# Scores of the pooled attention as 64-row products of even and odd tokens, with that order of tokens kept to the store

## The chip, the cores and the metric

The kernel runs on one core of a Trainium2 chip. The metric is the device time of one execution in microseconds (us). The core's engines are TensorE (PE in the profile, with PEld for its weight loads), VectorE (DVE), ScalarE (ACT), GpSimd (POOL) and SyncE (SP), whose queue issues all the DMA transfers here. Each engine works its own instructions in the order in which the program gives them.

## The reference

Eight batches of eight heads attend from 576 queries (64 dimensions) to 72 keys and values, each the mean of eight neighbours. The result, 4608 tokens by 512, goes through two dense layers with a squared ReLU between them.

```python
k_p = k.reshape(B, H, Sp, pool, D).mean(axis=3)
v_p = v.reshape(B, H, Sp, pool, D).mean(axis=3)
scores = scale * np.matmul(q, k_p.transpose(0, 1, 3, 2))
scores = scores - np.max(scores, axis=-1, keepdims=True)
attn = np.exp(scores)
attn = attn / (np.sum(attn, axis=-1, keepdims=True) + 1e-09)
attn_out = np.matmul(attn, v_p)
x = attn_out.transpose(0, 2, 1, 3).reshape(B * S, H * D)
h = np.maximum(x @ w_in, 0.0)          # 512 -> 2048
out = h * h @ w_out                    # 2048 -> 512
```

## The kernel before

The 4608 tokens are worked in 12 chunks of CH = 384. As a batch has 576 tokens, chunks 1, 4, 7 and 10 hold tokens of two batches (two segments of 192 in `segments`, lines 289 to 296), the others of one.

The main loop (lines 684 to 705) runs over 16 blocks of 128 hidden features for each chunk, in steps (c, fc). In step s TensorE gets twelve h products of 384 columns (`hidden`, line 502), then what the attention has for this step, then nine o products of 512 columns for the block two steps back (`project`, line 539; the lag is LAG = 2). Products of float32 accuracy are made from three products of fp32r parts, high times high, high times low and low times high; `split` (lines 127 to 129) makes the parts, the high one by a copy on ACT, the low one by a subtraction on DVE. Chunk 0, and the scores and the av products, use plain float32 operands.

The attention of a chunk is done for four pairs of heads, spread over the steps of the chunks before it (STEADY, line 87, gives the first step of each pair and the offsets of its stages from there). From chunk 2 on a pair's stages are these:

- `transpose_q` (line 309): four TensorE transposes put q of both heads into one PSUM bank `qps`, two neighbouring tokens at a time, so that the even token of each two stands on partitions 0 to 63 and the odd one on 64 to 127. The `then` part (lines 319 to 331) is the split: for each parity ACT copies the high part to its own 64 partitions of `st` and DVE writes the low part to the other 64. In `st` each token then has a column of 128 rows, half of it high and half low, in the order of the sequence.
- `scores` (line 335), one step later: for each head the products of `st` with `kl` and `kh`, the transposed pooled keys, which stand on both halves of the partitions. A product over 128 rows so sums the high and the low half. The scores of head i go to bank i of `sps`, 72 keys by 384 tokens, and ACT copies them to `sc`.
- `exponents` and the four stages behind it (lines 359 to 397): GpSimd takes maxima and sums over the 72 keys, ACT the exponentials, and the sums go over DRAM to be inverted in a compact form; `fetch_reciprocals` (line 392) broadcasts them from DRAM to the 64 partitions of each head in `rb`.
- `weigh_values` (line 472), eight steps after the transposes: `av` is the product of the exponents with the pooled values, the two heads on two halves of the output columns of the array; DVE multiplies it with `rb` and `split` makes `xh` and `xl`, the chunk's tokens for the h products.

At the end of a chunk `store` (lines 552 to 556) copies three tiles of 128 tokens out of PSUM and sends each with one DMA transfer to consecutive rows of the output.

In one step the order on TensorE is h, transposes and scores, av, o. Every transpose of q from chunk 3 on falls into a step with an av; the scores stand alone between the last h and the first o. The scores of chunks 0 and 1 are made otherwise (`token_scores`, line 408): in float32, with the tokens as stationary operand and 64 rows for each parity.

The lines that a sentence can't say are these of `scores`, line 343 and 344, the products that the change replaces:

```python
for j, kk in enumerate((kl, kh)):
    PE.matmul(ss[i][:SP_, o:o + n], lhsT=kk[:, h * SP_:(h + 1) * SP_], rhs=st[:, i, o:o + n], start=j == 0, stop=j == 1)
```

Of the kernel before, what the change touches and what calls it, by code (L numbers as in the profile page):

```python
# [9 lines left out]
F32 = mybir.dt.float32  # L10
# [4 lines left out]
ALU = mybir.AluOpType  # L15
# [22 lines left out]
def pooled_attn_relu2_ffn(  # L38
# [16 lines left out]
    PE, DVE, ACT, GP, SP = (InOrder(tc, e) for e in (nc.tensor, nc.vector, nc.scalar, nc.gpsimd, nc.sync))  # L55
    B, H, S, D = q.shape
# [3 lines left out]
    P = 128  # L60
    POOL = 8
    SP_ = S // POOL
# [3 lines left out]
    CH = 384  # L66
    QT = 96
    NQ = CH // QT
# [32 lines left out]
    ps_a = ctx.enter_context(tc.tile_pool(name="ps_a", bufs=3, space=bass.MemoryType.PSUM))  # L101
# [9 lines left out]
    for n in range(0, P, 32):  # L111
        rows = slice(n, n + 32)
# [3 lines left out]
    dma = SP.dma_start  # L116
# [10 lines left out]
    def split(hi, lo, src, eng=None):  # L127
        ACT.copy(hi, src)
        (eng or DVE).tensor_tensor(lo, src, hi.bitcast(F32), op=ALU.subtract)
# [5 lines left out]
    def w_tile(dt, name):  # L135
        return wts.tile([P, 2, 512], dt, name=name, tag="w", bufs=2 * NFC + 1)

    halves = {}

    def half_tile(kind, name):  # L140

        if kind not in halves:
            halves[kind] = w_tile(F32, name)
            return halves[kind][:, 0, :]
        return halves.pop(kind)[:, 1, :]
# [35 lines left out]
    kv, kf, loaded = {}, {}, {}  # L181
# [107 lines left out]
    def segments(c):  # L289
        t, segs = c * CH, []  # L290
        while t < (c + 1) * CH:
            b = t // S
            n = min((b + 1) * S, (c + 1) * CH) - t
            segs.append((b, t - c * CH, n))
            t += n
        return segs
# [12 lines left out]
    def transpose_q(c, p):  # L309


        pt = ps_a.tile([P, 512], F32, name=f"qps_{c}_{p}", tag="a")
        blocks = pt[:, :CH].rearrange("p (i t s) -> p i t s", i=2, s=QT)
        qt = loaded.pop(("q", c, p))
        for i in range(2):
            for t in range(NQ // 2):
                PE.transpose(blocks[:, i, t, :], qt[:, i, t * 2 * D:(t + 1) * 2 * D], ident[:QT, :QT])

        def then():
            if c < 2:  # L320
                st = live[c, p] = half_tile("s", f"st_{c}_{p}")[:, :CH]
                ACT.copy(st, pt[:, :CH])
                return
            st = live[c, p] = sb.tile([P, 2, CH], F32R, name=f"st_{c}_{p}", tag="st", bufs=STB)
            order = "p i (s t two) -> p i t s two" if len(segments(c)) == 1 else "p i (t s two) -> p i t s two"
            cols = st.rearrange(order, two=2, s=QT)
            halves = [(slice(i * D, (i + 1) * D), slice((1 - i) * D, (2 - i) * D), i) for i in range(2)]
            for own, oth, i in halves:
                ACT.copy(cols[own, :, :, :, i], blocks[own])
            for own, oth, i in halves:  # L330
                DVE.tensor_tensor(cols[oth, :, :, :, i], blocks[own], cols[own, :, :, :, i].bitcast(F32), op=ALU.subtract)

        return then

    def scores(c, p):

        st = live.pop((c, p))
        ss = [ps_a.tile([P, 512], F32, name=f"sps_{c}_{p}_{i}", tag="a") for i in range(2)]
        for i in range(2):
            h = 2 * p + i  # L340
            for b, o, n in segments(c):
                kh, kl, _ = kv[b]
                for j, kk in enumerate((kl, kh)):
                    PE.matmul(ss[i][:SP_, o:o + n], lhsT=kk[:, h * SP_:(h + 1) * SP_], rhs=st[:, i, o:o + n], start=j == 0, stop=j == 1)

        def then():
            sc = sb.tile([SP_, 2, CH], F32, name=f"sc_{c}_{p}", tag="sc", bufs=SCB)
            mx = reduced("mx", c, p)
            for i in range(2):
                ACT.copy(sc[:, i, :], ss[i][:SP_, :CH])  # L350
                GP.partition_all_reduce(mx[i], sc[:, i, :], channels=SP_, reduce_op=bass_isa.ReduceOp.max)
            live[c, p] = (sc, mx)

        return then

    def reduced(kind, c, p):
        return [sb.tile([SP_, CH], F32, name=f"{kind}_{c}_{p}_{i}", tag="mx", bufs=3) for i in range(2)]
# [34 lines left out]
    def fetch_reciprocals(c, p):  # L392
        sc, rd = live.pop((c, p))
        rb = sb.tile([P, CH], F32, name=f"rb_{c}_{p}", tag="rb", bufs=2)
        for i in range(2):
            dma(rb[i * D:(i + 1) * D, :], rd[i:i + 1, :].broadcast_to([D, CH]))
        live[c, p] = (sc, rb)


# [72 lines left out]
    def weigh_values(c, p):  # L472

        if p == 0 and c == 0:
            x0.extend(w_tile(F32, f"x_{c}_{i}")[:, :, :CH] for i in range(2))
        elif p == 0:
            xts[c] = (sb.tile([P, NPAIR, CH], F32R, name=f"xh_{c}", tag="xh", bufs=2),
                      sb.tile([P, NPAIR, CH], F32R, name=f"xl_{c}", tag="xl", bufs=2))
        sc, rb = live.pop((c, p))
        av = ps_a.tile([P, 512], F32, name=f"av_{c}_{p}", tag="a")  # L480
        for b, o, n in segments(c):
            for i in range(2):
                PE.matmul(av[i * D:(i + 1) * D, o:o + n], lhsT=kv[b][2][:, 2 * p + i, :], rhs=sc[:, i, o:o + n],
                                 start=True, stop=True)

        def then():
            if c == 0:
                ACT.copy(x0[p // 2][:, p % 2, :], av[:, :CH])
                return
            xh, xl = xts[c]  # L490
            if c == 1:
                split(xh[:, p, :], xl[:, p, :], av[:, :CH])
                return
            DVE.tensor_tensor(rb, av[:, :CH], rb, op=ALU.mult)
            split(xh[:, p, :], xl[:, p, :], rb)

        return then
# [41 lines left out]
    def project(c, fc):  # L539
        if fc == 0:  # L540
            accs[c] = [ps_o.tile([P, 512], F32, name=f"o_{c}_{t}", tag=f"o{t}") for t in range(NTT)]
        g, key = gts.pop((c, fc)), ("o", fc)
        for t in range(NTT):
            tt = slice(t * P, (t + 1) * P)
            if c == 0:
                prods = [(g[:, tt], wf[key])]
            else:
                prods = [(g[x][:, tt], wt[key][:, w, :]) for x, w in ((0, 0), (0, 1), (1, 0))]
            for i, (a, w) in enumerate(prods):
                PE.matmul(accs[c][t], lhsT=a, rhs=w, start=fc == 0 and i == 0, stop=fc == NFC - 1 and i == len(prods) - 1)  # L550

        def store():
            for t in range(NTT):
                ob = sb.tile([P, DM], F32, name=f"ob_{c}_{t}", tag="ob", bufs=OB)
                ACT.copy(ob, accs[c][t])
                dma(out[c * CH + t * P:c * CH + (t + 1) * P, :], ob)

        return store if fc == NFC - 1 else None

# [58 lines left out]
    for p in range(NPAIR):  # L618
        token_normalise(0, p)
        after = [token_scores(0, p + 2)] if p + 2 < NPAIR else []  # L620
        if p:
            weigh_values(0, p - 1)()
        keep_busy(IDLE[1])
        if p == 2:
            for key in first_keys:
                magnitude(key)
        token_turn(0, p)()
        for f in after:
            f()
    to_float32(*first_keys)  # L630
    weigh_values(0, NPAIR - 1)()
    for hf in range(2):
        at(0, transpose_k, 1, hf)
# [4 lines left out]
    t = 1e9  # L638
    for key in reversed(keys):
        t = min(t - 1 / RATE, need[key] - 1 - MARGIN)  # L640
# [23 lines left out]

    ready = {0, 1}
    stages = (transpose_q, scores, exponents, send_sums, fetch_sums, reciprocals, fetch_reciprocals, weigh_values)
    for c in range(1, NCH):
        first, offsets = EARLY if c == 1 else STEADY
# [5 lines left out]
        for p in range(NPAIR):  # L674
            s = c * NFC + first[p]
# [5 lines left out]

    last = (to_float32, split_weights)
    on_pe = (transpose_k, transpose_q, scores, token_scores, token_turn, weigh_values)
    for s in range(-PRO, len(steps) + LAG):
        todo = work.get(s, [])
# [50 lines left out]
```

## Time and profile before

| what | us |
|---|---|
| median of three runs | 964.42 |
| lowest and highest of them | 963.8, 966.72 |
| the profiled execution | 964.33 |
| its span, from the first to the last instruction | 962.6 |
| TensorE matmuls busy | 946.1 |
| VectorE busy | 615.0 |
| ScalarE busy | 451.5 |
| GpSimd busy | 348.8 |

The profile is taken in one execution; "busy" is the time in which an engine has at least one instruction under way. TensorE's instructions overlap in its pipeline and their ends are modelled, so that what one of them costs is read from the distance between two starts, not from its duration. A row of the timeline has the start, the time to the end of its last instruction, the engine, the operation, output and inputs by their names in the program (buffer numbers left out), rows and columns, and how many equal instructions are merged; the idle time before it and what ended it stand in brackets. Line L34 is the helper that issues every instruction, so that rows are told apart by the names of the tiles.

### The profile page before, as it was taken

To read this page: it belongs to the slowest core of one execution; us is meant where nothing else is said; L and a number is where in the kernel's file an instruction comes from. 1 tells how busy PE (TensorE), PEld (TensorE's weight loads), DVE (VectorE), ACT (ScalarE), POOL (GpSimd) and SP (SyncE) were. 2 spreads that over 40 slices of the span, in tenths; PEclk is the share of its full clock that TensorE was granted. 3 is DMA by queue.
4 is the path that set the end of the run, shared out by engine and by line. 5 is a ranking of instruction groups with operands and counts; after the bars stand their busy time and mean duration, and the time that the engine had idled before them with its cause. 6 is when DMAs were issued, how large, how long until landed. Compare 5 with 4: busy or idle time off the path is not lost.

```text
span 962.6 us, 13481 instructions
## 1 busy us (share of the span) xinstructions
PE 946.1 (98%) x4944; PEld 803.6 (83%) x4944; DVE 615.0 (64%) x1028; ACT 451.5 (47%) x909; POOL 348.8 (36%) x215
## 2 busy tenths in 40 slices
PE   7899999999999999999999999999999999999998
PEld 6456668888888888888888888888888888888997
DVE  7889886667865566677765656767776565453221
ACT  3789776754444344444344344434443434532322
POOL 3800144444444434344353444344443534440000
PEclk9799999999999999999999999999999999999999
DMA  9963112113112112112112112112211110100000
GB/s 256 319 237 116 61 33 78 35 50 98 52 31 77 32 34 67 48 52 82 52 44 77 30 35 79 38 30 69 82 50 39 68 32 18 58 10 9 33 1 34
DMA packets 51651, 63.65 MB, mean 66 GB/s; under 512 B 13936, under 2 KB 32192, under 8 KB 51584
## 3 DMA queue, kind: packets, MB, share of 16 engines
q1 hardware_dynamic: 51584, 62.78, 21.2%
q8 instruction: 39, 0.64, 0.3%
q14 instruction: 28, 0.23, 0.1%
HBM read 53.08 MB, written 9.68 MB: 65 GB/s over the span
## 4 chain that ended last, share of the span: by engine, by line
PE 88%; DVE 5%; DMA 4%; ACT 2%; issue 1%; SPq 0%; ACTq 0%; DVEq 0%
PE o L34 41%; PE h L34 39%; PE av L34 3%; PE sps L34 3%; DVE wf_o L34 2%; DVE wf_i L34 1%; PE qps L34 1%; DMA raw_o<-in_moe_w_out_dram 1%; DMA v<-in_v_dram 1%; DMA k<-in_k_dram 1%; ACT te L34 1%; DMA vv<-in_v_dram 1%; DMA raw_i<-in_moe_w_in_dram 1%; DVE tm L34 1%; DVE w_i L34 1%
## 5 line engine op out<-in xcount | busy, mean ns | idle before, releaser
L34 PE MATMUL h<-xh,w_i 128*128 128x384 f32 x1488 | 416.9, 341 | 0.0
L34 PE MATMUL o<-w_o,gh 128*128 128x512 f32 x1056 | 334.8, 398 | 0.0
L34 PEld LDWEIGHTS h<-xh,w_i 128*128 128x128 f32 x1488 | 272.8, 188 | 10.6 <-issue 1.4
L34 POOL PARTITION_ALL_REDUCE tot<-sc x80 | 201.4, 2564 | 210.1 <-issue 199.6
L34 PE MATMUL h<-xl,w_i 128*128 128x384 f32 x744 | 249.9, 336 | 0.0
L34 PEld LDWEIGHTS o<-w_o,gh 128*128 128x128 f32 x1056 | 192.4, 188 | 51.9 <-issue 16.5
L34 POOL PARTITION_ALL_REDUCE mx<-sc x80 | 117.8, 1519 | 287.1 <-ACT sc L34 287.1
L34 DVE TENSOR_TENSOR gl<-r,gh 128x384 fp32r<-128x384 f32 x176 | 143.5, 815 | 109.1 <-ACT gh L34 108.9
L34 PE MATMUL o<-w_o,gl 128*128 128x512 f32 x528 | 209.1, 396 | 0.0
L34 DVE TENSOR_TENSOR r<-r 128x384 f32<-128x384 f32 x160 | 105.6, 660 | 109.1 <-ACT r L34 108.8
L34 ACT CAST gh<-r 128x384 fp32r<-128x384 f32 x176 | 90.4, 514 | 150.3 <-DVE r L34 149.8
L34 PEld LDWEIGHTS h<-xl,w_i 128*128 128x128 f32 x744 | 139.7, 188 | 10.6 <-issue 2.9
L34 ACT ACTIVATE r<-h 128x384 f32<-128x384 f32 x192 | 94.2, 491 | 100.5 <-PE h L34 99.1
L34 PEld LDWEIGHTS o<-w_o,gl 128*128 128x128 f32 x528 | 99.1, 188 | 22.1
L34 DVE TENSOR_TENSOR st<-qps,st 64x384 fp32r<-64x384 f32 x80 | 60.8, 760 | 59.1 <-ACT st L34 58.3
L34 ACT CAST st<-qps 64x384 fp32r<-64x384 f32 x80 | 59.5, 744 | 56.9 <-PE qps L34 56.5
L34 ACT CAST xh<-rb 128x384 fp32r<-128x384 f32 x40 | 20.5, 513 | 94.6 <-DVE rb L34 94.6
L34 ACT ACTIVATE sc<-sc 72x384 f32<-72x384 f32 x80 | 39.7, 525 | 46.4 <-DVE sc L34 46.4
L34 DVE TENSOR_REDUCE vp<-v 72x64 f32<-72x512 f32 x48 | 51.0, 1062 | 0.0
L34 PE MATMUL av<-sc,vp 72*64 72x384 f32 (+1 forms) x256 | 45.6, 436 | 3.6 <-ACT sc L34 2.1
L34 PE MATMUL o<-wf_o,r 128*128 128x512 f32 x96 | 44.4, 598 | 0.0
L34 DVE TENSOR_REDUCE kp<-k 96x64 f32<-96x512 f32 x42 | 43.8, 1043 | 0.2 <-DMA k<-in_k_dram 0.2
(82 smaller groups left out, 702.1 us busy)
## 6 DMA issues: line engine op xcount, KB each, us to landing
k<-in_k_dram SPq DMA_DIRECT2D x48, 192.0 KB
out_dram<-ob SPq DMA_DIRECT2D x36, 256.0 KB
raw_i<-in_moe_w_in_dram SPq DMA_DIRECT2D x16, 512.0 KB
raw_o<-in_moe_w_out_dram SPq DMA_DIRECT2D x16, 512.0 KB
v<-in_v_dram SPq DMA_DIRECT2D x56, 144.0 KB
rb<-rd SPq DMA_DIRECT2D x80, 96.0 KB
q<-in_q_dram SPq DMA_DIRECT2D x30, 192.0 KB
q<-in_q_dram SPq DMA_DIRECT2D x32, 96.0 KB
```

What stands on the lines that cost most here:

```text
L34: return lambda *a, **k: self.tc.keep_in_program_order(f(*a, **k))
```

## The change

From chunk 2 on the split of q keeps the parities where the transposes put them: `st` gets the high parts in its first half and the low ones in its second, each over 128 partitions, even tokens on partitions 0 to 63 and odd ones on 64 to 127. The scores become products over 64 rows, three terms for each parity (high keys by low queries, low by high, high by high), alternating between the two halves of the array; bank j of `sps` now holds parity j, with both heads one behind the other. A product has 192 columns in a chunk of one batch and 96 in one of two. The order of tokens (even ones, then odd ones, each by transposed blocks) stays through the softmax, av and both layers: `rb` is fetched in that order, av reads and writes it with longer access patterns, and the store sends each tile of 128 rows in two pieces of rows that lie 4 tokens apart (2 in chunks of two batches).

```diff
--- before.py
+++ after.py
@@ -322,26 +322,24 @@
                 ACT.copy(st, pt[:, :CH])
                 return
             st = live[c, p] = sb.tile([P, 2, CH], F32R, name=f"st_{c}_{p}", tag="st", bufs=STB)
-            order = "p i (s t two) -> p i t s two" if len(segments(c)) == 1 else "p i (t s two) -> p i t s two"
-            cols = st.rearrange(order, two=2, s=QT)
-            halves = [(slice(i * D, (i + 1) * D), slice((1 - i) * D, (2 - i) * D), i) for i in range(2)]
-            for own, oth, i in halves:
-                ACT.copy(cols[own, :, :, :, i], blocks[own])
-            for own, oth, i in halves:
-                DVE.tensor_tensor(cols[oth, :, :, :, i], blocks[own], cols[own, :, :, :, i].bitcast(F32), op=ALU.subtract)
+            split(st[:, 0], st[:, 1], pt[:, :CH])
 
         return then
 
     def scores(c, p):
 
         st = live.pop((c, p))
-        ss = [ps_a.tile([P, 512], F32, name=f"sps_{c}_{p}_{i}", tag="a") for i in range(2)]
-        for i in range(2):
-            h = 2 * p + i
-            for b, o, n in segments(c):
-                kh, kl, _ = kv[b]
-                for j, kk in enumerate((kl, kh)):
-                    PE.matmul(ss[i][:SP_, o:o + n], lhsT=kk[:, h * SP_:(h + 1) * SP_], rhs=st[:, i, o:o + n], start=j == 0, stop=j == 1)
+        ss = [ps_a.tile([P, 512], F32, name=f"sps_{c}_{p}_{j}", tag="a") for j in range(2)]
+        n = CH // 2 // len(segments(c))
+        for h in (2 * p, 2 * p + 1):
+            for t, (b, _, _) in enumerate(segments(c)):
+                o = h % 2 * (CH // 2) + t * n
+                for k, (w, x) in enumerate(((0, 1), (1, 0), (0, 0))):
+                    for j in range(2):
+
+                        two = slice(j * D, (j + 1) * D)
+                        PE.matmul(ss[j][:SP_, o:o + n], lhsT=kv[b][w][two, h * SP_:(h + 1) * SP_], rhs=st[two, x, o:o + n],
+                                  start=k == 0, stop=k == 2)
 
         def then():
             sc = sb.tile([SP_, 2, CH], F32, name=f"sc_{c}_{p}", tag="sc", bufs=SCB)
@@ -393,7 +391,8 @@
         sc, rd = live.pop((c, p))
         rb = sb.tile([P, CH], F32, name=f"rb_{c}_{p}", tag="rb", bufs=2)
         for i in range(2):
-            dma(rb[i * D:(i + 1) * D, :], rd[i:i + 1, :].broadcast_to([D, CH]))
+            dma(rb[i * D:(i + 1) * D, :].rearrange("p (two n) -> p two n", two=2),
+                rd.rearrange("two (i n) -> i two n", i=2)[i:i + 1].broadcast_to([D, 2, CH // 2]))
         live[c, p] = (sc, rb)
 
 
@@ -478,10 +477,14 @@
                       sb.tile([P, NPAIR, CH], F32R, name=f"xl_{c}", tag="xl", bufs=2))
         sc, rb = live.pop((c, p))
         av = ps_a.tile([P, 512], F32, name=f"av_{c}_{p}", tag="a")
-        for b, o, n in segments(c):
+        m = CH // 2 // len(segments(c))
+        for t, (b, o, n) in enumerate(segments(c)):
             for i in range(2):
-                PE.matmul(av[i * D:(i + 1) * D, o:o + n], lhsT=kv[b][2][:, 2 * p + i, :], rhs=sc[:, i, o:o + n],
-                                 start=True, stop=True)
+                x, y = av[i * D:(i + 1) * D, o:o + n], sc[:, i, o:o + n]
+                if c > 1:
+                    x = av[i * D:(i + 1) * D, :CH].rearrange("p (two n) -> p two n", two=2)[:, :, t * m:(t + 1) * m]
+                    y = sc.rearrange("p two (i n) -> p i two n", i=2)[:, i, :, t * m:(t + 1) * m]
+                PE.matmul(x, lhsT=kv[b][2][:, 2 * p + i, :], rhs=y, start=True, stop=True)
 
         def then():
             if c == 0:
@@ -553,7 +556,15 @@
             for t in range(NTT):
                 ob = sb.tile([P, DM], F32, name=f"ob_{c}_{t}", tag="ob", bufs=OB)
                 ACT.copy(ob, accs[c][t])
-                dma(out[c * CH + t * P:c * CH + (t + 1) * P, :], ob)
+                rows = out[c * CH:(c + 1) * CH]
+                if c < 2:
+                    dma(rows[t * P:(t + 1) * P, :], ob)
+                    continue
+                rows = rows.rearrange("(s t two) d -> two t s d" if len(segments(c)) == 1 else "(t s two) d -> two t s d", t=2, two=2)
+                for n in range(NQ):
+                    lo, hi = max(n * QT, t * P), min((n + 1) * QT, (t + 1) * P)
+                    if lo < hi:
+                        dma(rows[n // 2, n % 2, lo - n * QT:hi - n * QT, :], ob[lo - t * P:hi - t * P, :])
 
         return store if fc == NFC - 1 else None
```

## The prediction

> **What bounds the kernel now.** I read the page first (span and busy times), then the sums by stretch, then TensorE's timeline around the instructions that the change replaces.
>
> ```profile
> span 962.6 us, 13481 instructions
> PE 946.1 (98%) x4944; PEld 803.6 (83%) x4944; DVE 615.0 (64%) x1028; ACT 451.5 (47%) x909; POOL 348.8 (36%) x215
> core 0: us, PE busy (x) PEld busy (x) DVE busy (x) ACT busy (x) POOL busy (x), PEclk, DMA share, GB/s
> 145.00:865.00 720.00, 720.00 (x3792) 630.74 (x3790) 468.93 (x739) 323.54 (x642) 304.58 (x153) 1.00 0.17 52
> ```
>
> The first two rows are the page's, the last two the sums by stretch. In the 720 us from 145 to 865 TensorE is busy for all 720 at the full granted clock (1.00), while DVE works 469 us and ACT 324. So in this stretch the time is the sum of TensorE's spacings and nothing else: whatever the change takes from DVE and ACT there is worth nothing, and each nanosecond between two matmul starts counts in full. Busy time is modelled and pipelined matmuls overlap, so I use differences of start times.
>
> **The score products before.** Two views: the tile view of the score tile, and TensorE's timeline around one pair of heads, first in a chunk inside one batch, then in one that crosses batches.
>
> ```profile
> L34 PE MATMUL sps<-st,kl x104: 249/334/341, 107.9 to 849.9; 128*72 128x384 f32 x56, 128*72 128x192 f32 x48
> ...
> 169.61 0.34 PE L34 MATMUL sps<-st,kl 128*72 128x384 f32 x1
> ...
> 170.32 0.63 PE L34 MATMUL o<-w_o,gh 128*128 128x512 f32 x2
> 170.78 0.39 PE L34 MATMUL o<-w_o,gl 128*128 128x512 f32 x1
> ...
> 264.41 0.25 PE L34 MATMUL sps<-st,kl 128*72 128x192 f32 x1
> ...
> 265.11 0.65 PE L34 MATMUL o<-w_o,gh 128*128 128x512 f32 x2
> 265.60 0.40 PE L34 MATMUL o<-w_o,gl 128*128 128x512 f32 x1
> ```
>
> Each pair has as many kl as kh matmuls: four of 384 columns in a one-batch chunk (56 kl, two each: 28 pairs), eight of 192 in chunks 4, 7 and 10 (48 kl, four each: 12 pairs). The four take 170.32 - 169.61 = 0.71 us; elsewhere 0.70, I use 0.705. The eight take 265.11 - 264.41 = 0.70, and the two o products behind them 0.49 where 0.46 is usual (170.78 - 170.32), so 0.74. One matmul of 192 columns is 0.70 / 8 = 0.0875.
>
> **What replaces them.** Per pair: two heads, three terms, two halves of the array. In a one-batch chunk that is six rounds of two 64-row matmuls with 192 columns; in the others twelve rounds with 96. The weights are 72 columns each time. Two prices are needed: a round, and the way into the half-array form and out of it, because the blocks stand alone between h and o, which use all 128 rows. The trace has both. The scores of chunks 0 and 1 already run in 64-row halves, and the av products run in two column halves:
>
> ```profile
> 99.09 0.34 PE L34 MATMUL h<-xh,w_i 128*128 128x384 f32 x1
> 99.36 0.90 PE L34 MATMUL sps<-kf,st 64*96 64x72 f32 x16
> 100.19 0.55 PE L34 MATMUL qps<-ident,q 96*128 96x96 f32 x4
> 99.35 0.76 PEld L34 LDWEIGHTS sps<-kf,st 64*96 64x96 f32 x16 [0.25 <-issue]
> L34 PE MATMUL sps<-kf,st x128: 245/245/300, 10.3 to 100.0; 64*96 64x72 f32 x128
> L34 PEld LDWEIGHTS sps<-kf,st x128: 156/162/162, 10.3 to 99.9; 64*96 64x96 f32 x128
> ...
> 212.37 0.62 PE L34 MATMUL o<-w_o,gh 128*128 128x512 f32 x2
> 212.82 0.40 PE L34 MATMUL o<-w_o,gl 128*128 128x512 f32 x1
> ...
> 220.74 0.49 PE L34 MATMUL qps<-ident,q 96*128 96x96 f32 x4
> 221.17 0.87 PE L34 MATMUL av<-sc,vp 72*64 72x384 f32 x4
> 221.96 0.73 PE L34 MATMUL o<-w_o,gh 128*128 128x512 f32 x2
> 222.53 0.40 PE L34 MATMUL o<-w_o,gl 128*128 128x512 f32 x1
> ...
> L34 PE MATMUL av<-sc,vp x256: 326/432/902, 24.1 to 881.0; 72*64 72x384 f32 x64, 72*64 72x192 f32 x64
> ```
>
> A round. The 16 half-array matmuls are eight rounds. Their weight loads take 0.76 us, the last one alone 0.162, so (0.76 - 0.162) / 7 = 0.085 from load to load. The matmuls say the same: (0.90 - 0.245 - 0.055 for the first, which lasts 300 and not 245) / 7 = 0.086. Sixteen matmuls one after another at that spacing would take 1.37 us, and the block is over in 0.83: the halves do run side by side. With 72 moving columns and 96 weight columns I take this row as bound by its loads, 0.085 / 96 = 0.89 ns a column, so 0.064 for 72 columns (an estimate). A round with 192 columns is then bound by its columns, 0.0875 as in full rows; one with 96 (0.044) by its loads, 0.064. Bounds: for 96 columns 0.044 to the 0.085 measured; for 192 from 0.0875 to 0.11, that plus what 0.064 of load may stick out as the loads of this row stick out of its own columns. I take 0.0875 and 0.064.
>
> The way in and out. From h to the first half-array matmul 99.36 - 99.09 = 0.27 instead of the 0.17 of an h of 384 columns: 0.10 lost. The first matmul waits another 0.055 for its weights. The eight rounds end at 99.36 + 0.055 + 8 x 0.085 = 100.095, but qps starts at 100.19: 0.095 lost on leaving. At av the same: its four qps should be over after 4 x 0.082 ((0.49 - 0.245) / 3) = 0.33 and av comes after 0.43; the av block takes 0.79 of which its columns are 0.64 (the shortest av matmul, of 192 columns, is 326 and the longer form 486 where nothing delays it, so 0.16 per 192 columns, and here two rounds of 384); and the first two o behind it take 0.57 instead of 0.45, as the first waits for weights that could not be loaded ahead. Sum 0.10 + 0.15 + 0.12 = 0.37; by the half-array row with the same o behind it 0.10 + 0.055 + 0.095 + 0.11 = 0.36. I take 0.36, with 0.30 (a qps-like start behind it, 0.055 instead of 0.11) and 0.38 as ends.
>
> The Trainium skill, "TensorEngine Tiling (Array Packing)", section Key Properties, says that changing the tiling mode drains TensorE; the trace agrees, with the 0.095 to 0.10 at each change above. The same page's table of theoretical speedups gives up to twofold for a contraction of 64 or less; by that alone the six rounds would halve the twelve matmuls and the sum would be the "free passage" rival below.
>
> **The sum on TensorE.** One-batch pair: 6 x 0.0875 + 0.36 = 0.885 against 0.705, +0.18; 28 of them +5.0 us. Two-batch pair: 12 x 0.064 + 0.36 = 1.13 against 0.74, +0.39; 12 of them +4.7. Together +9.7. The columns saved are real (in a one-batch pair 1152 pass instead of 1536) but the passage costs twice what they bring.
>
> **ACT and DVE.** The split of q becomes one copy and one subtraction over 128 partitions.
>
> ```profile
> 102.94 1.71 ACT L34 CAST st<-qps 64x384 fp32r<-64x384 f32 x2
> 104.67 0.48 ACT L34 CAST xh<-av 128x384 fp32r<-128x384 f32 x1
> 104.68 1.77 DVE L34 TENSOR_TENSOR st<-qps,st 64x384 fp32r<-64x384 f32 x2 [2.91 <-ACT st L34]
> 106.48 0.56 DVE L34 TENSOR_TENSOR xl<-av,xh 128x384 fp32r<-128x384 f32 x1
> 114.14 0.63 PE L34 MATMUL pps<-ident,te 96*72 96x96 f32 x4 [0.76 <-DVE te L34]
> ```
>
> The same split of av (128 x 384 out of PSUM) takes 0.48 and 0.56, so each pair saves about 1.2 us on each engine. Behind 145 us it is hidden under TensorE, as the first view shows, and stays worth nothing. Ahead of it there is one TensorE wait behind DVE after the first such split: at 113.05 h starts, 0.17 later the next could, and pps starts at 114.14, 0.92 late, on a DVE queue that was running without a break since this st. It may lose all or nothing of this; with about 2 us less in front of it I take 0.7 of 0.9 as gone.
>
> **Queues.** The store of a chunk becomes six transfers instead of three, and the two broadcasts of the reciprocals are cut into pieces of half the length.
>
> ```profile
> L34 SPq DMA_DIRECT2D out_dram<-ob x36: 332/362/1040, 145.2 to 959.8; - x36
> 958.40 1.72 SPq L34 DMA_DIRECT2D out_dram<-ob  x3
> L34 SPq DMA_DIRECT2D rb<-rd x80: 450/552/597, 139.8 to 874.5; - x80
> L34 DVE TENSOR_TENSOR rb<-av,rb x40: 557/558/558, 149.9 to 881.6; 128x384 f32<-128x384 f32 x40
> ```
>
> An issue takes SP 0.33 us and the copies in front of the three last ones are 0.69 apart (1.72 less one issue, over two), so the extra issues of the first two tiles fit between; the last tile's second issue ends the run about 0.35 later (0 if the smaller transfer lands as much sooner, 0.5 at most). Mid-run the 30 added issues stand ahead of the next chunk's loads and sums on SP's queue, some 1 us per chunk. The broadcast is issued at 139.8 and first used at 149.9: 10 us of cover for two issues of 0.55, so even twice that is hidden. If it were not, DVE's rb would hold up gl behind it on the same queue, and o two steps later.
>
> Total: +9.7 - 0.7 + 0.35 = +9.35. The profiled execution took 964.33 us (1.7 outside the span), the median of the runs is 964.42, so the two can be used alike: **973.7 us**. Low end: passage 0.30, rounds 0.0875 and 0.044, all of the 0.9 gained: 28 x 0.12 + 12 x 0.09 - 0.9 = +3.6, 968. High end: passage 0.38, rounds 0.11 and 0.085, nothing gained: 28 x 0.335 + 12 x 0.66 + 0.4 = +17.7, 982.
>
> **Rivals.**
> Free passage (faster). If going from 128 rows to two halves and back drains nothing for these formats, only columns count: 28 x (0.525 - 0.705) + 12 x (0.77 - 0.74) = -4.7, with the small terms -5.0: 959.3. It decides at a passage of 0.12 us, where 40 passages eat those 4.7. Against it: every change of form in the rows above costs 0.30 or more. For it: these rows are fp32, the new products fp32r, which no row shows in halves.
> Loads that wait. If the weights of a half can only be loaded when that half's matmul is over, a round is 0.0875 + 0.064 = 0.15 or 0.044 + 0.064 = 0.108: 28 x 0.555 + 12 x 0.92 = +26.6, with the small terms 990.5. Against it the 0.085 from load to load while matmuls of the same half run; for it, that row may be waiting in just this way, with shorter parts than I think. The Trainium skill, "TensorE: Matmul & The Clock Gate", Part 3, The mechanism, has such a rule: a load overlaps matmuls in flight only where the row group differs.
> No side by side. If the halves take turns in fp32r, the change does not do what it says: 12 x 0.0875 = 1.05 and 24 x 0.064 = 1.54 per pair, 28 x 0.705 + 12 x 1.16 = +33.7, with the small terms 997.6. Against it the 0.83 us for 16 matmuls.
>
> **How the numbers follow.** The forecast gets 0.80, loads that wait 0.06, no side by side 0.06, free passage 0.05, and a passage near its turning point 0.03 (no change: within 0.3%, about 2.9 us, which is what a measurement of this kernel can tell). The range 968 to 982 is the forecast's own and leaves out 0.20. Faster 0.05, same 0.03, slower 0.92.
>
> **What would show it.** Right: in the timeline of the changed kernel h to first score 0.27, six rounds about 0.0875 apart and twelve about 0.064, 0.18 from the last round to o, the first o 0.11 longer; TensorE still without a wait from 145 us on; the wait at pps smaller; DVE and ACT each some 40 us less busy. Wrong: rounds at 0.15, or 0.17 from h to the first score, or a TensorE wait that names rb, st or a store. The most uncertain number is the round of 96 columns, since no row has fp32r loads of 72 columns with so little to hide behind.

## The result: 1% slower, and the profile after

The changed kernel takes 975.52 us (median of 4 runs, 974.08 to 976.28), the kernel before 965.57 in the runs beside it (4 runs, 963.80 to 967.81). The ratio is 1.011, with a 95% interval of 1.009 to 1.013. The profiled execution of the changed kernel took 974.08 us, 972.4 of it in the span, against 964.33 and 962.6 before: 9.8 us more.

First the page and the sums by stretch of the changed kernel, in the columns of the rows of before (busy time of each engine with its instructions, granted clock, DMA).

```profile
span 972.4 us, 14205 instructions
PE 955.3 (98%) x5360; PEld 802.9 (83%) x5360; DVE 572.5 (59%) x988; ACT 410.8 (42%) x869; POOL 345.7 (36%) x215
145.00:873.00 728.00, 728.00 (x4185) 629.32 (x4182) 428.07 (x698) 283.69 (x600) 299.00 (x152) 1.00 0.18 50
```

DVE and ACT lost 42 and 41 us of work, and TensorE is busy for all 728 of 728 us, at the full clock, as before. So in this stretch the change has made TensorE's own sequence longer. Its timeline shows where: first a block in a one-batch chunk, then one in a chunk of two batches, each from the last h to the first o products.

```profile
168.67 0.34 PE L34 MATMUL h<-xh,w_i 128*128 128x384 f32 x1
168.93 0.31 PE L34 MATMUL sps<-st,kh 64*72 64x192 f32 x2
169.08 0.25 PE L34 MATMUL sps<-st,kl 64*72 64x192 f32 x2
169.17 0.34 PE L34 MATMUL sps<-st,kh 64*72 64x192 f32 x4
169.35 0.25 PE L34 MATMUL sps<-st,kl 64*72 64x192 f32 x2
169.44 0.25 PE L34 MATMUL sps<-st,kh 64*72 64x192 f32 x2
169.62 0.72 PE L34 MATMUL o<-w_o,gh 128*128 128x512 f32 x2
170.18 0.39 PE L34 MATMUL o<-w_o,gl 128*128 128x512 f32 x1
...
264.33 0.34 PE L34 MATMUL h<-xh,w_i 128*128 128x384 f32 x1
264.59 0.27 PE L34 MATMUL sps<-st,kh 64*72 64x96 f32 x2
264.70 0.23 PE L34 MATMUL sps<-st,kl 64*72 64x96 f32 x2
...
265.35 0.23 PE L34 MATMUL sps<-st,kh 64*72 64x96 f32 x2
265.51 0.73 PE L34 MATMUL o<-w_o,gh 128*128 128x512 f32 x2
266.08 0.40 PE L34 MATMUL o<-w_o,gl 128*128 128x512 f32 x1
```

The matmuls of a round are two in a row (x2), side by side; 169.35 to 169.44 is one round of 192 columns, 0.09. From h to the first score pass 0.26 instead of 0.17, from the last round to o 0.18 instead of the 0.09 of its columns, and the first two o take 0.56 instead of 0.46. From the first score to the third o it was 1.17 (170.78 - 169.61) and is 1.25; with the 0.09 at the entry +0.17. In the two-batch chunk 1.19 has become 1.49, with the entry +0.39.

Two more places differ, one early and one at the very end. The rows are the timeline of TensorE near 113 us, its last matmul, and the issues of the last stores on SP's queue.

```profile
112.96 0.33 PE L34 MATMUL h<-xh,w_i 128*128 128x384 f32 x1
113.13 0.82 PE L34 MATMUL pps<-ident,te 96*72 96x96 f32 x8
...
966.82 0.40 PE L34 MATMUL o<-w_o,gl 128*128 128x512 f32 x1
966.48 3.09 SPq L34 DMA_DIRECT2D out_dram<-ob  x6
```

The pps transposes follow h at once; before, they stood 0.92 us late behind DVE. The last matmul starts at 966.82, before the change at 958.74: 8.08 later. From it to the end of the span there were 962.6 - 958.74 = 3.9 us and are now 972.4 - 966.82 = 5.6. So the 9.8 us are 8.1 on TensorE (in which the 0.9 of pps is already deducted) and 1.7 behind it.

### The profile page after: what moved, and what is told of

Read it like the earlier page. It is cut to its first block, busy times and chain, and to the rows that moved or that the text cites. A ratio compares the mean times of both kernels' runs of the same rounds, so it can differ in the third digit from the quotient of the medians.

```text
span 972.4 us, 14205 instructions
## 1 busy us (share of the span) xinstructions
PE 955.3 (98%) x5360; PEld 802.9 (83%) x5360; DVE 572.5 (59%) x988; ACT 410.8 (42%) x869; POOL 345.7 (36%) x215
## 4 chain that ended last, share of the span: by engine, by line
PE 92%; DVE 3%; DMA 2%; ACT 1%; issue 1%; SPq 0%; DVEq 0%; ACTq 0%
PE o L34 42%; PE h L34 40%; PE av L34 4%; PE sps L34 3%; PE qps L34 1%; DVE wf_o L34 1%; DVE wf_i L34 1%; DMA raw_i<-in_moe_w_in_dram 1%; DMA vv<-in_v_dram 1%; SPq L34 0%; ACT te L34 0%; PE vps L34 0%; DVE tm L34 0%; DMA q<-in_q_dram 0%; DVE w_i L34 0%
## 5 line engine op out<-in xcount | busy, mean ns | idle before, releaser
L34 PE MATMUL o<-w_o,gh 128*128 128x512 f32 x1056 | 338.8, 402 | 0.0
L34 POOL PARTITION_ALL_REDUCE mx<-sc x80 | 114.6, 1479 | 292.5 <-ACT sc L34 292.5
L34 ACT COPY sc<-sps 72x384 f32<-72x384 f32 x80 | 34.1, 476 | 78.1 <-PE sps L34 78.1
L34 ACT CAST st<-qps 128x384 fp32r<-128x384 f32 x40 | 19.1, 478 | 62.0 <-PE qps L34 62.0
```

The source lines that it names most:

```text
L34: return lambda *a, **k: self.tc.keep_in_program_order(f(*a, **k))
```

## The experiments

Each run is the changed kernel with the edit shown. The questions were three: is it the passage into half-array form and out of it that costs, or the rounds; why is the end later; and what are the shorter queues of ACT and DVE worth.

**The same rounds without the passage.** The half-array products become half as many over all 128 rows, so that the number of rounds, the columns and the weight columns stay.

```diff
-                for k, (w, x) in enumerate(((0, 1), (1, 0), (0, 0))):
-                    for j in range(2):
-
-                        two = slice(j * D, (j + 1) * D)
-                        PE.matmul(ss[j][:SP_, o:o + n], lhsT=kv[b][w][two, h * SP_:(h + 1) * SP_], rhs=st[two, x, o:o + n],
-                                  start=k == 0, stop=k == 2)
+                for j, k, w, x in ((0, 0, 0, 1), (0, 1, 1, 0), (1, 1, 0, 0)):
+                    PE.matmul(ss[j][:SP_, o:o + n], lhsT=kv[b][w][:, h * SP_:(h + 1) * SP_], rhs=st[:, x, o:o + n],
+                              start=k == 0 or j == 1, stop=k == 1)
```

> The changed kernel with three products per head and segment over all 128 rows in place of the six over 64 rows: as many rounds, the same weight and moving columns, no change of form (left out: the parities are not kept apart, the scores are sums over both). Theory, the cost is the passage into halves and back: a one-batch block falls from 0.89 us to 6 x 0.0875 = 0.53, a two-batch block from 1.12 to between 0.53 and 0.77, so 28 x 0.36 + 12 x (0.35 to 0.6) = 14 to 17 us less than the changed kernel: 958 to 961 us. Rival, the rounds of small products are what costs and the passage little: within 3 us of the changed kernel, 972 to 976.

It took 961.44 us (span 959.7). The timeline of a one-batch block, and the ends of a two-batch one:

```profile
167.30 0.34 PE L34 MATMUL h<-xh,w_i 128*128 128x384 f32 x1
167.48 0.25 PE L34 MATMUL sps<-st,kh 128*72 128x192 f32 x1
...
167.92 0.25 PE L34 MATMUL sps<-st,kh 128*72 128x192 f32 x1
168.01 0.65 PE L34 MATMUL o<-w_o,gh 128*128 128x512 f32 x2
168.49 0.40 PE L34 MATMUL o<-w_o,gl 128*128 128x512 f32 x1
...
261.54 0.21 PE L34 MATMUL sps<-st,kh 128*72 128x96 f32 x1
...
262.30 0.69 PE L34 MATMUL o<-w_o,gh 128*128 128x512 f32 x2
```

Six rounds take 168.01 - 167.48 = 0.53, the entry 0.18 and the two o 0.48: the block with its edges is 0.32 shorter than in halves, at the same rounds. The span is 12.7 us shorter, which is 12.7 / 40 = 0.32 a passage. The lower end of the forecast was 14: in the two-batch chunks I had thought that rounds of 96 columns might take only the 0.044 of their columns, and in full rows they take (262.30 - 261.54) / 12 = 0.063, as in halves (0.064 by the next run). A round is one matmul here and two in halves, so its price does not go by the number of matmuls; it fits the estimate for one load of 72 weight columns. The rival, 972 to 976, is out.

**Every round twice.** The passages stay and the rounds double.

```diff
-                for k, (w, x) in enumerate(((0, 1), (1, 0), (0, 0))):
+                for k, (w, x) in enumerate(2 * ((0, 1), (1, 0), (0, 0))):
...
-                                  start=k == 0, stop=k == 2)
+                                  start=k == 0, stop=k == 5)
```

> The changed kernel with every round of the scores done twice inside its block, the passages as they were (the scores come out doubled). Theory: 28 blocks get 6 rounds of 0.083 to 0.0875 more, 12 get 12 of 0.061 to 0.064: +14 to 15 and +8.8 to 9.2, together +23 to 24 us, 998 to 1000. Rival, the loads of a half wait for its matmul and a round costs 0.15 and 0.11: +25 and +16, 1016.

It took 999.13 us (span 997.4). One block of each kind, from the first score to o:

```profile
170.83 0.31 PE L34 MATMUL sps<-st,kh 64*72 64x192 f32 x2
...
172.04 0.74 PE L34 MATMUL o<-w_o,gh 128*128 128x512 f32 x2
...
269.21 0.27 PE L34 MATMUL sps<-st,kh 64*72 64x96 f32 x2
...
270.90 0.74 PE L34 MATMUL o<-w_o,gh 128*128 128x512 f32 x2
```

Six more rounds of 192 columns add 1.21 - 0.69 = 0.52 to a block, twelve of 96 add 1.69 - 0.92 = 0.77: 0.087 and 0.064 a round. What is left of the changed block beyond its rounds and beside h and o at their usual distance is the passage: 0.95 from h to o and 0.10 on the first o, less the 0.17 of h and 0.52 for the rounds, 0.36. Rounds whose loads waited for the matmul of the same half would have added 0.15 and 0.11 each, so that rival is out. The Trainium skill, "TensorE: Matmul & The Clock Gate", Part 3, The mechanism, says that a load overlaps matmuls in flight only where the row group differs; taken by itself, that sentence does not hold here. The same section also lets a load into the background weight buffer go ahead; that would fit these rounds, and no run here can show such a buffer.

**One return fewer.** Transposes and scores of chunks 3 to 11 go one step earlier, so that the scores stand in one step with an av block; av is worked with column halves, and the array goes from row halves to column halves without full rows between.

```diff
     STEADY = ((-22, -18, -14, -10), (0, 1, 3, 4, 5, 6, 7, 8))
+    LATER = ((-23, -19, -15, -11), (0, 1, 3, 4, 5, 6, 7, 9))
...
-        first, offsets = EARLY if c == 1 else STEADY
+        first, offsets = EARLY if c == 1 else STEADY if c == 2 else LATER
...
-        return [sb.tile([SP_, CH], F32, name=f"{kind}_{c}_{p}_{i}", tag="mx", bufs=3) for i in range(2)]
+        return [sb.tile([SP_, CH], F32, name=f"{kind}_{c}_{p}_{i}", tag="mx", bufs=4) for i in range(2)]
```

> The changed kernel with transposes and scores of chunks 3 to 11 one step earlier, so that the scores stand in one step with an av block, right ahead of it (one buffer more for the maxima). All products are the same; from scores to av the array goes straight from row halves to column halves. Theory of the passage: one return to full rows with its weight load that cannot be hidden (0.095 + 0.106 = 0.20 us) goes for 36 pairs: 7.2 us less than the changed kernel, 968.3 us. Rival, the cost belongs to each block whatever stands beside it: 975.5. Second rival, three banks of scores and av in one step make TensorE wait for ACT: up to 0.5 us a pair, 980 or more.

The median of 10 runs is 968.8 us (967.08 to 978.27), 1.0062 of the kernel before (interval 1.0038 to 1.0086), against 1.011 for the changed kernel beside its own runs.

```profile
415.55 0.25 PE L34 MATMUL sps<-st,kh 64*72 64x192 f32 x2
415.73 0.86 PE L34 MATMUL av<-sc,vp 72*64 72x384 f32 x4
416.53 0.73 PE L34 MATMUL o<-w_o,gh 128*128 128x512 f32 x2
417.10 0.40 PE L34 MATMUL o<-w_o,gl 128*128 128x512 f32 x1
```

From the last round to av it takes 0.18 again, so this change of form, too, costs its 0.09; what is gone is one way back with its o that waits for weights. From the same h product near 175 us to the last matmul TensorE's sequence is 7.0 us shorter than in the changed kernel, 7.2 were forecast. No wait on three banks shows. The same products in the same numbers, only put side by side, take back 7 of the 10 us: the passage is the cost.

**The end.** Four runs take the store apart. One transfer per tile to consecutive rows:

```diff
-                rows = out[c * CH:(c + 1) * CH]
...
-                        dma(rows[n // 2, n % 2, lo - n * QT:hi - n * QT, :], ob[lo - t * P:hi - t * P, :])
+                dma(out[c * CH + t * P:c * CH + (t + 1) * P, :], ob)
```

> The changed kernel with one transfer per tile to consecutive rows, as before (left out: the rows of a chunk stay in the order of the kernel). Theory, the end lost 1.7 us to six issues in a row on SP: the time from the last matmul to the end of the span goes back from 5.5 to 3.9 us, TensorE's sequence stays as it is: 973.8 us or 1.7 less than the changed kernel. Rival, the end is later because the scattered rows land more slowly: the end stays within 0.5 us of 5.5 without this order only if it is something else still.

973.7 us; the end is 972.0 - 968.10 = 3.9 behind the last matmul, the old value. That the whole comes within 0.1 of the forecast 973.8 is luck: TensorE's sequence, which was to stay as it is, has its last matmul 1.3 later than in the profile of the changed kernel, after a fall of the clock that is told below.

The last two of the six issues from ACT's queue:

```diff
-                        dma(rows[n // 2, n % 2, lo - n * QT:hi - n * QT, :], ob[lo - t * P:hi - t * P, :])
+                        (ACT.dma_start if c == NCH - 1 and t == NTT - 1 else dma)(rows[n // 2, n % 2, lo - n * QT:hi - n * QT, :], ob[lo - t * P:hi - t * P, :])
```

> The changed kernel with the two pieces of the very last tile issued by ACT behind its last copy, the other four by SP. Theory, the six issues on one queue set the end: the last issue ends 0.7 us earlier and the time from the last matmul to the end of the span falls from 5.5 to 4.8 us. Rival, the landing of scattered rows sets it: 5.5 as before.

974.05 us; the rows are the last matmul and the issues on both queues.

```profile
966.91 0.40 PE L34 MATMUL o<-w_o,gl 128*128 128x512 f32 x1
967.96 0.89 ACTq L34 DMA_DIRECT2D out_dram<-ob  x2
966.57 2.00 SPq L34 DMA_DIRECT2D out_dram<-ob  x4
```

The last issue is over at 968.85, 1.9 behind the last matmul instead of 2.75 (969.57 in the changed kernel), and yet the end comes 972.3 - 966.91 = 5.4 behind it instead of 5.6. So the end hardly follows the last issue, and my theory fell: an issue that is over 0.8 earlier gains 0.2 of the 1.7. Two runs then parted the two things left, the cutting into pieces and the distance between the rows. Six pieces to consecutive rows:

```diff
-                        dma(rows[n // 2, n % 2, lo - n * QT:hi - n * QT, :], ob[lo - t * P:hi - t * P, :])
+                        dma(out[c * CH + lo:c * CH + hi, :], ob[lo - t * P:hi - t * P, :])
```

> The changed kernel with six transfers per chunk as they are (32 to 96 rows each) but to consecutive rows of the output (left out: the order of the rows). The end of the changed kernel is 5.5 us behind the last matmul, with one transfer per tile 3.9; with two queues for the six issues it was 5.4, so the issues are not what it waits for. If the cutting into pieces is the cause: 5.3 to 5.6 again. If the distance between the rows is the cause: 4.2 to 4.6, the old end and the later issues.

And one transfer per tile to every third row:

```diff
-                if c < 2:
...
-                        dma(rows[n // 2, n % 2, lo - n * QT:hi - n * QT, :], ob[lo - t * P:hi - t * P, :])
+                dma(rows[t * P:(t + 1) * P, :] if c < 2 else rows.rearrange("(s t) d -> t s d", t=NTT)[t], ob)
```

> The changed kernel with one transfer per tile of 128 rows, each to every third row of the chunk's output (left out: the order of the rows). If the distance between the rows sets the end: 4.8 us or more from the last matmul to the end. If the cutting into pieces does: 3.9, as with consecutive rows.

They took 973.7 and 972.64 us. Their sums by stretch, from the first to the last of the 384 rows of the last chunk that land, ahead of them the same of the kernel before and of the changed one (the last two numbers are the share of the DMA engines that is busy and GB/s), then the last matmul of each of the two runs:

```profile
959.23:961.43 2.20, 0.00 (x0) 0.00 (x0) 0.00 (x0) 0.53 (x1) 0.00 (x0) 0.97 0.92 358
967.30:971.06 3.76, 0.00 (x0) 0.00 (x0) 0.00 (x0) 0.54 (x1) 0.00 (x0) 1.00 0.74 209
966.80:970.70 3.90, 0.00 (x0) 0.00 (x0) 0.00 (x0) 0.54 (x1) 0.00 (x0) 1.00 0.72 201
967.50:969.75 2.25, 0.00 (x0) 0.00 (x0) 0.00 (x0) 0.56 (x1) 0.00 (x0) 1.00 0.90 350
...
966.32 0.40 PE L34 MATMUL o<-w_o,gl 128*128 128x512 f32 x1
967.04 0.40 PE L34 MATMUL o<-w_o,gl 128*128 128x512 f32 x1
```

Pieces to consecutive rows land at 201 GB/s and end 972.0 - 966.32 = 5.7 behind the last matmul; whole tiles to every third row land at 350 GB/s and end 970.9 - 967.04 = 3.9 behind it. So a distance of three rows costs nothing here, and the cutting costs all of the 1.7 us. By the same rows the DMA engines are busy for 0.92 x 2.20 = 2.0 us with the old store and 0.74 x 3.76 = 2.8 us with the new one, for the same bytes, and stand idle for 0.2 and 1.0 us of the landing. So half of what the landing lost is slower movement and half is gaps. Why transfers of 32 to 96 rows behave so, no run shows.

**What the shorter queues are worth.** Near 113 us, the subtraction of the very first split is repeated, first four and then eight times:

```diff
             split(st[:, 0], st[:, 1], pt[:, :CH])
+            for _ in range(4 if (c, p) == (2, 0) else 0):
+                DVE.tensor_tensor(st[:, 1], pt[:, :CH], st[:, 0].bitcast(F32), op=ALU.subtract)
```

> The changed kernel in which DVE does the subtraction of the very first split (chunk 2, first pair of heads) four times more, 4 x 0.56 = 2.2 us, writing the same values. Theory, the 0.9 us that TensorE no longer waits before the pps transposes near 113 us came from the shorter DVE queue: the wait is back, pps starts 0.9 us or more after the last h ahead of it could end, and all that follows is 0.9 to 1.1 us later than in the changed kernel. Rival, the wait went by chance or through ACT: pps follows h at once, as in the changed kernel.

978.51 us, and no wait at pps: a miss. DVE's timeline of the changed kernel says why.

```profile
103.20 0.56 DVE L34 TENSOR_TENSOR st<-qps,st 128x384 fp32r<-128x384 f32 x1 [1.70 <-ACT st L34]
...
109.45 1.14 DVE L34 TENSOR_TENSOR te<-te,tm 96x288 f32<-96x288 f32 x2
```

te is ready at 110.59 and pps starts at 113.13: a lead of 2.5 us, more than the 2.2 put in. I had sized the run by the 0.9 us of the wait and not by the lead that has taken its place. The span of this run is 4.4 us longer than that of the changed kernel, but for other reasons: 2.8 had come together before 100 us, where the mean granted clock was 0.86 against 0.95 in the changed kernel, and 1.4 in a fall of the clock that is told below. Therefore eight:

> As the run with four more subtractions behind the very first split, with eight, 4.5 us. In the changed kernel the te that pps needs is ready 2.5 us ahead of pps, and the four used up 2.3 of it. Theory of the queue: te now comes 2 us after the point at which pps could start, TensorE waits for DVE te near 113 us for about 2 us (0.5 if the clock falls to half near 102 us, which holds TensorE up for 1.5). Rival, te does not hang on this queue: no wait.

976.96 us. TensorE's waits between 103 and 120 us, and its timeline there:

```profile
PE sps L34 <- DVE st L34: 0.9, 1, 0.9
PE pps L34 <- DVE te L34: 0.8, 1, 0.8
PE h L34 <- DVE w_i L34: 0.8, 1, 0.8
...
114.23 0.34 PE L34 MATMUL h<-xh,w_i 128*128 128x384 f32 x1
115.34 0.89 PE L34 MATMUL pps<-ident,te 96*72 96x96 f32 x7 [0.76 <-DVE te L34]
```

The wait for te is back, after two others behind the same queue (the scores for their own st, and h for the weights that DVE prepares): 2.5 us in all, so that pps itself is only 0.9 late and not the forecast 2. DVE's queue sets this place.

Everywhere else the relief should be worth nothing. From chunk 3 on the split is done three times:

```diff
             split(st[:, 0], st[:, 1], pt[:, :CH])
+            for _ in range(2 if c > 2 else 0):
+                split(st[:, 0], st[:, 1], pt[:, :CH])
```

> The changed kernel in which the split of q is done three times instead of once from chunk 3 on, with the same values: per pair some 1.0 us more on ACT and 1.1 on DVE, about what the change saved (36 pairs: ACT +35, DVE +40 us busy). Theory, what the change takes from ACT and DVE is worth nothing under a TensorE that never waits: TensorE's sequence from 145 us on is the same to 0.1 us, 975.5 us. Rival, the shorter ACT and DVE queues give something back that the sum by TensorE's spacings hides: 1 us or more slower.

978.42 us. DVE works 608.6 us in it and ACT 442.3, nearly as much as before the change, and TensorE's waits from 143 us to the end are these:

```profile
PE sps L34 <- DVE st L34: 0.7, 3, 0.2
```

Three scores of forty wait for their own, threefold split, which costs 0.3 us each; from one score block to the next, all others are as far apart as in the changed kernel, to 0.01 us. Of the 4.3 us by which the span is longer 3.3 came from the clock near 102 us, told below. So some 70 us of work more on ACT and DVE cost TensorE 0.9, by the longer chain of one split and not by the queues. The forecast of 0.1 was too low for that reason, and the sum comes near the 1 us of the rival; but the cost lies at three splits that are on the path themselves, and the claim that the saved work has no worth in this stretch holds.

**The best that the experiments point to.** The change in one-batch chunks alone and not in the last, with one passage:

```diff
+    NEW = (2, 3, 5, 6, 8, 9)
...
-                if c > 1:
+                if c in NEW:
```

with the old split, products, broadcast and store for the other chunks from 2 on, and the moved steps of the run with one passage.

> The change in chunks 2, 3, 5, 6, 8 and 9 only (one batch, and not the last, so that the end is the old one), the others as before; from chunk 3 on the scores one step before av as in the run with one passage. By the sum: 4 pairs of chunk 2 at +0.18, 20 pairs at +0.18 - 0.20, and the 0.9 to 1.1 us at pps gained: -0.6 to -0.8 us against before, 963.5 us, which the measurement cannot tell from no change. Rival, the mix of two orders or the moved steps cost something of their own: 966 or more.

The median of 12 runs is 964.37 us (962.26 to 970.78), 1.0008 of the kernel before, with an interval of 0.9990 to 1.0026. Nothing is lost and nothing gained that such times can show. The timeline shows a little more. The rows are the first h behind the first changed block, and the last matmul:

```profile
112.02 0.73 PE L34 MATMUL h<-xh,w_i 128*128 128x384 f32 x1
...
958.89 0.40 PE L34 MATMUL o<-w_o,gl 128*128 128x512 f32 x1
```

From one to the other TensorE's sequence takes 846.87 us; in the kernel before the same h starts at 110.73 and the same stretch takes 958.74 - 110.73 = 848.01. So 1.1 us are gained there, 0.9 of them at pps, and with the 0.18 of the first block some 1.0 against the forecast 0.6 to 0.8. The profiled execution is no faster for it, as it had come to this h 1.3 later. No version here that computes the whole result has a shorter median than the kernel before by more than the measurement can tell.

## Why the prediction was right, and where it was not

The forecast was 973.7, range 968 to 982; measured were 975.52, and for the profiled execution +9.8 us against +9.35 forecast. The mechanism held. That the total came so close is in part luck: the end was 1.35 too small, and the other terms together 0.9 too large.

- That TensorE's spacings alone make the time from 145 us on was right: 728 of 728 us busy after, and no wait of TensorE.
- The rounds, 0.0875 and 0.064, were measured as 0.087 and 0.064 by doubling them. That two halves run side by side, and that a round of 96 columns takes the time of a load and not of its columns, held for fp32r as the fp32 rows had it.
- The passage, 0.36, was 0.36 by the remainder and 0.32 against full-row rounds, whose own first o also starts late (0.48 for two). The price came from a block that the kernel already had, av, whose edges showed the same four parts.
- Per pair +0.18 and +0.39 were forecast, +0.17 and +0.39 are in the rows. The sum of 9.7 was 9.3: 8.1 at the last matmul, plus 0.9 gained at pps, plus 0.3 by which this execution was ahead at the h in front of the first block.
- The wait at pps: 0.7 of 0.9 taken as gained, all 0.9 came, and behind it a lead of 2.5 us.
- The end was the term mis-sized: +0.35 with 0.5 "at most", measured +1.7. The step that failed is that "the extra issues of the first two tiles fit between" and that the smaller transfers land no later. The sum had taken 0.33 us for an issue; the six took 3.09 us in a row, and the pieces land at 209 GB/s instead of 358. With two queues for the issues the end came only 0.2 earlier, so most of it is the landing.
- The free passage, loads that wait and turns taken instead of side by side are out by the first two runs: 0.32 to 0.36 is paid, rounds do not grow by a load, and 0.087 is one column stream and not two. The drain at each change of form, which the Trainium skill gives in "TensorEngine Tiling (Array Packing)", Key Properties, agrees with the 0.09 at every entry and exit, fp32r included.

## What to carry to other kernels

Before small products are packed into halves of the array, price the way in and out from a block that already does so: here 0.36 us, as much as two full matmuls of 384 columns, for 0.18 us of columns saved. If such blocks are wanted, put them side by side, since the return to full rows with its exposed weight load is the dear half. And an order of rows that has to be undone in the last store should keep each transfer at full tiles: whole tiles to every third row ended as early here as whole tiles to consecutive rows.

## What the runs showed of the hardware that was not expected

A transfer of fewer rows is no cheaper: SP's six issues of 32 to 96 rows took 3.09 us where three of 128 rows, paced by the copies ahead of them, took 1.72, and the rows landed at 201 to 209 GB/s instead of 350 to 358, in consecutive and in spread rows alike (every third row for whole tiles, every fourth for pieces).

TensorE waits 1.3 to 1.6 us for te between 100 and 105 us in every profile. In four of the thirteen the granted clock then falls from 1.00 to 0.50; that the wait is the cause, no run shows. The sums from 100 to 110 us of the changed kernel, of the run with plain stores and of the run with the threefold split (the clock is the third number from the end):

```profile
100.00:110.00 10.00, 8.48 (x48) 5.41 (x47) 8.13 (x20) 6.93 (x20) 0.91 (x1) 1.00 0.23 73
100.00:110.00 10.00, 8.48 (x41) 5.23 (x40) 7.83 (x20) 5.75 (x17) 0.00 (x0) 0.83 0.20 69
100.00:110.00 10.00, 8.50 (x26) 4.51 (x26) 7.75 (x20) 5.49 (x16) 0.00 (x0) 0.66 0.22 73
```

A mean of 0.83 over 10 us is 3.4 us at half, 0.66 is 6.8 us. At 0.83 the sequence behind it is 1.4 to 1.7 us later (three runs) and at 0.66 3.3. The first chunk has such a fall in every profile, of varying length: the mean clock of the first 100 us is 0.95 in the changed kernel and 0.86 in the run with four more subtractions. So a single time of these kernels cannot show a term of one microsecond, and such terms were read from the timelines.
